# Attention with relative bias and a low-rank mixer: value products of the first three groups woven between scores in a new order, batch 0's remainder loads cast on the way, padding set sooner

## Chip, cores, metric

The kernel runs on one core of a Trainium2 chip. The metric is device microseconds of one execution. A comparison always has the kernel before beside it on the same chip, in alternating rounds.

## The reference, cut to what matters

```python
# q, k, v: (8 batches, 8 heads, 576 positions, 64)
scores = scale * q @ k^T + bias_table[bucket(|i - j|)]      # bucket saturates at distance 128
attn   = exp(scores - max) / (sum + 1e-9)
x      = (attn @ v) as (batch, 576, 512)
h      = (x^T @ U @ V)^T ;  u = x + h                        # U: (576, 32), V: (32, 576)
out    = u + relu(u @ w_ch1) @ w_ch2                         # 512 -> 2048 -> 512
```

The kernel treats two heads as a "pair" and one pair of one batch as a "group": group 0 to 3 are batch 0, group 4 begins batch 1. The 576 positions are four tiles of 128 and a remainder of 64. The bias is a factor exp(bias), read from table rows that only matter near the diagonal.

## The kernel before: the parts that count here

The main loop starts at group 4 and interleaves attention with the two large products of earlier batches. In front of it stands a prologue, written by hand, for batch 0. In the timelines of this document each engine runs its instructions in the order in which the program emits them, so one that waits holds all that stand behind it.

```python
def kts(g, *ks):          # scores of key tiles ks, then ScalarE's exponentials of them
def rem_scores(g):        # scores with the remainder of q and of k
def bands(g, *ks):        # VectorE: multiply the near-diagonal part by exp(bias)
def pvs(g, *ks):          # value products of both heads; ks=4 is the remainder and opens the sum
def normalise(g):         # VectorE: divide by the row sums, into x
def mix_t(g, copy), mix_ut(g, copy)     # x^T U, and u transposed
def first_transposes(pr, srcs, copies): # TensorE: 8 + 8 transposes of a pair's q and k, two copies out
def warm(n):              # n idle products of the identity
...
# loads on GpSimd, in this order, behind the table rows 0:
load_eb(0, nc.gpsimd)                        # waits until the table row is written
load_rem(0, 2)                               # v of batch 0: remainder,
for t in range(NKT): load_main(0, 2, t)      #   four tiles of 128 KB
qk0[3] = [first_qk(which, 3) for which in range(2)]      # pair 3's q and k
...
# the prologue, middle part
rem_scores(1)
more_loads()                                 # first of it: load_eb(3) on the SP queue
bands(0, 4, 0, 1, 2, 3)
kts(1, 2); warm(3); kts(1, 3)
reverse_eb(1); bands(1, 4, 0, 1, 2, 3)
rem_scores(2); kts(2, 0)
pvs(0, 4, 0, 1); kts(2, 1)
pvs(0, 2);       kts(2, 2)
pvs(0, 3); normalise(0); kts(2, 3)
first_transposes(3, qk0.pop(3), (nc.vector.tensor_copy, nc.scalar.copy))   # pair 3
first_rem_transposes(3)
pvs(1, 4, 0); rem_scores(3); pvs(1, 1, 2, 3); normalise(1); kts(3, 0)
...
```

The softmax here doesn't subtract the row's maximum and nothing guards it: scores larger than these inputs give would overflow.

## Time and profile before

| | |
|---|---|
| time | 392.95 us median of 3 (392.76 to 394.05) |
| TensorE busy | 96% of the span, 84% of the chain that ended last |
| VectorE, ScalarE, GpSimd busy | 76%, 52%, 33% |
| first remainder score of group 4 (the loop's start) | 35.58 us |
| span of the profiled execution | 392.6 us, granted clock 0.993 |

The busy shares are those of the whole span and say nothing about the prologue, which is 9% of it. To read the prologue, take each engine's timeline from 0 to 40 us: the bracket behind a line gives the idle time before it and who ended it. The lines are in the prediction.

### The profile page before, as it was taken

The page shows a single profiled execution, that of the slowest core. Times are in us where ns is not written, and L with a number is a line of the kernel's source. Part 1 is how long each engine was busy: PE and PEld are TensorE (multiplying, and loading weights), DVE is VectorE, ACT ScalarE, POOL GpSimd, SP SyncE. Part 2 cuts the span into 40 slices and gives each one's busy share as a digit, 9 for nine tenths or more (in the row PEclk, how much of TensorE's full clock was granted, in tenths as well). Part 3 has the DMA queues.
Part 4 walks back from the last instruction along what each step waited for, and adds up shares of the span by engine and source line. Part 5 has one row for each costly group of instructions (what it writes and reads, how often), then busy time and mean ns, then how long its engine had stood idle before and what let it go on. Part 6 is the DMA issues. An engine that isn't in the chain of part 4 may idle for free.

```text
span 392.6 us, 10145 instructions
## 1 busy us (share of the span) xinstructions
PE 376.6 (96%) x4126; PEld 250.9 (64%) x4161; DVE 299.6 (76%) x659; ACT 205.9 (52%) x312; POOL 129.5 (33%) x187
## 2 busy tenths in 40 slices
PE   7789999999999999999999999999999999999995
PEld 5366555555568656875588557855687569568474
DVE  7856898878897788877887888767876897465573
ACT  5977555565655676546755655566545650220310
POOL 4998917554554055404550335213000000000000
PEclk9989999999999999999999999999999999999998
DMA  7999999999999599978999798979003003401103
GB/s 135 180 96 168 158 202 115 135 102 140 179 80 96 124 160 84 106 131 148 105 82 134 145 110 65 141 140 142 3 16 122 15 15 28 121 1 55 53 2 107
DMA packets 163478, 40.66 MB, mean 104 GB/s; under 512 B 151568, under 2 KB 159032, under 8 KB 163432
## 3 DMA queue, kind: packets, MB, share of 16 engines
q0 software_dynamic: 110304, 18.24, 63.9%
q1 hardware_dynamic: 51864, 20.86, 25.4%
q10 hardware_dynamic: 1264, 0.92, 1.0%
q8 instruction: 32, 0.52, 0.5%
q14 instruction: 14, 0.11, 0.1%
HBM read 37.84 MB, written 9.45 MB: 120 GB/s over the span
## 4 chain that ended last, share of the span: by engine, by line
PE 84%; DVE 10%; ACT 2%; issue 1%; DMA 1%; SPq 0%; ACTq 0%; DVEq 0%
PE acc L410 28%; PE acc L539 26%; PE o L801 11%; PE sc L707 8%; PE acc L462 3%; DVE g L421 3%; PE acc L874 2%; PE sc L725 2%; DVE p_sb L777 2%; PE sc L746 1%; PE acc L681 1%; DMA stage<-in_q_dram 1%; DVE qkT L650 1%; DVE xp L827 1%; PE o L854 1%
## 5 line engine op out<-in xcount | busy, mean ns | idle before, releaser
L716 ACT ACTIVATE p_sb<-sc 128x1024 bf16<-128x1024 f32 (+1 forms) x125 | 120.3, 1015 | 97.2 <-PE sc L707 97.1
L410 PE MATMUL acc<-uT,w1b 128*128 128x512 bf16 x481 | 115.8, 380 | 2.2 <-issue 0.8
L410 PEld LDWEIGHTS <-w1b 128*128 128x128 bf16 x576 | 53.1, 98 | 68.7 <-issue 13.4
L421 DVE TENSOR_SCALAR g<-acc 128x512 f16<-128x512 f32 x97 | 64.8, 685 | 10.5 <-PE acc L410 9.6
L777 DVE TENSOR_TENSOR p_sb<-p_sb,eb 128x768 bf16<-128x768 bf16 (+4 forms) x156 | 65.5, 454 | 0.3 <-ACT p_sb L716 0.3
L801 PEld LDWEIGHTS <-p_sb 128*128 128x128 bf16 x1550 | 54.2, 98 | 4.8 <-issue 1.4
L539 PEld LDWEIGHTS <-g 128*128 128x128 f16 x512 | 48.7, 98 | 12.1 <-issue 5.5
L801 PE MATMUL o<-v_bf,p_sb 128*128 128x65 bf16 x1475 | 56.1, 193 | 0.3 <-DVE xp L827 0.3
L419 ACT ACTIVATE g<-acc 128x512 f16<-128x512 f32 x47 | 28.1, 598 | 46.3 <-PE acc L410 45.6
L539 PE MATMUL acc<-w2b,g 128*128 128x256 f16 x384 | 47.0, 273 | 0.1
L707 PE MATMUL sc<-qkT 64*128 64x512 bf16 x256 | 40.6, 385 | 1.4 <-ACT p_sb L716 0.9
L1147 POOL COPY gate<-xp 1x2 bf16<-1x2 bf16 x18 | 3.9, 214 | 114.3 <-DVE xp L827 114.3
L827 DVE TENSOR_TENSOR xp<-o,rcp 128x320 bf16<-128x320 f32 x60 | 29.5, 492 | 3.2
L539 PE MATMUL acc<-tw,stage 128*128 128x256 f16 x256 | 31.7, 273 | 0.0
L426 DVE TENSOR_TENSOR ob<-acc,u_tok 128x512 f32<-128x512 f32 x28 | 19.3, 688 | 13.5 <-PE acc L539 13.4
L275 POOL DMA_DIRECT2D v_bf<-in_v_dram x32 | 28.4, 926 | 0.3 <-issue 0.3
L882 DVE TENSOR_TENSOR u_tok<-acc,xp 128x512 bf16<-128x512 f32 x32 | 22.0, 686 | 8.5 <-PE acc L874 8.3
L539 PEld LDWEIGHTS <-stage 128*128 128x128 f16 x256 | 24.6, 98 | 4.0 <-issue 1.3
L558 DVE TENSOR_TENSOR ob<-acc,ob 128x512 f32<-128x512 f32 (+1 forms) x25 | 16.7, 667 | 11.6 <-PE acc L539 11.5
L757 ACT ACTIVATE p_sb<-sc 128x640 bf16<-128x640 f32 x31 | 21.7, 699 | 0.3 <-PE sc L749 0.3
L738 ACT ACTIVATE p_sb<-sc 128x512 bf16<-128x512 f32 x31 | 18.5, 597 | 4.1 <-PE sc L921 1.0
L275 POOL DMA_DIRECT2D qb<-in_k_dram x20 | 18.2, 909 | 1.6 <-issue 1.6
(126 smaller groups left out, 450.5 us busy)
## 6 DMA issues: line engine op xcount, KB each, us to landing
out_dram<-ob SPq DMA_DIRECT2D x16, 512.0 KB, 2.8
v_bf<-in_v_dram POOLq DMA_DIRECT2D x32, 128.0 KB, 5.6
qb<-in_q_dram POOLq DMA_DIRECT2D x23, 128.0 KB, 4.1
qb<-in_k_dram POOLq DMA_DIRECT2D x23, 128.0 KB, 4.2
w1b<-in_moe_w_ch_dram POOLq DMA_DIRECT2D x4, 512.0 KB, 7.0
w2b<-in_moe_w_ch_dram POOLq DMA_DIRECT2D x2, 1024.0 KB, 14.3
qb<-in_q_dram POOLq DMA_DIRECT2D x10, 64.0 KB, 5.5
qb<-in_k_dram POOLq DMA_DIRECT2D x10, 64.0 KB, 4.1
```

The costliest lines, as they stand in the source:

```text
L275: nc.gpsimd.dma_start(out=dst, in_=src[b, :, t * 128 : (t + 1) * 128, :].rearrange("h p d -> p h d"),)
L410: nc.tensor.matmul(gp_, lhsT=w1b[:, ct, nt * 128 : (nt + 1) * 128], rhs=rhs[:, ct, :], start=(ct == 0), stop=(ct == 3),)
L419: nc.scalar.activation(g[:, nt, :], gp_, AF.Relu)
L421: nc.vector.tensor_relu(out=g[:, nt, :], in_=gp_)
L539: nc.tensor.matmul(ps, lhsT=left[a](n)[:, t * 128 : t * 128 + 128], rhs=right[b](n), start=first and n == 0, stop=n == 7, skip_group_check ...
L707: nc.tensor.matmul(sp[:, hh, :], lhsT=kT[rows, i * 128 : (i + 1) * 128], rhs=qT[rows, 0:S0], start=True, stop=True,)
L716: nc.scalar.activation(P[:, i, hh, 0:S0], sp[:, hh, :], AF.Exp, scale=scale)
L757: nc.scalar.activation(P4[:, 0:SP], sp.rearrange("p a c -> p (a c)")[:, 0:SP], AF.Exp, scale=scale,)
L777: nc.vector.tensor_tensor(out=t, in0=t, in1=e, op=ALU.mult)
L801: nc.tensor.matmul(o[:, qt * 66 : qt * 66 + 65], lhsT=lhs[:, c0 : c0 + 128], rhs=rhs, start=(kt == NKT and qt == 0), stop=(kt == NKT - 1), ...
L827: nc.vector.tensor_tensor(out=xo[:, :, hh], in0=o[:, :, 0:64], in1=rbc, op=ALU.mult)
L882: nc.vector.tensor_tensor(out=u_tok[b % 3][:, pr, :, :], in0=hm.rearrange("p (t c) -> p t c", t=4), in1=x[:, 0:4, :], op=ALU.add,)
```

## The change

Its intent: let value products stand where TensorE waited for exponentials, take four VectorE casts and two fp32 loads out of the start, and put padding memsets on GpSimd in a wait it had anyway. The diff, cut to its core:

```diff
     first_load(1, 0, 2, k00, nc.scalar)
-    first_rem_load(0, nc.sync)
-    first_rem_load(1, nc.scalar)
     nc.scalar.activation(gmT[:, 0:1], negt31, AF.Exp)
     qk0[1] = [first_qk(which, 1) for which in range(2)]
+    load_rem(0, 0)
+    load_rem(0, 1)
     qk0[2] = [first_qk(which, 2) for which in range(2)]
@@
-    load_eb(0, nc.gpsimd)
+    load_eb(0)
@@
     setup_rest()
+    nc.gpsimd.dma_start(out=gate, in_=gp_dram[0:1, 0:2])
     load_rem(0, 2)
@@ casts and the order
     kts(0, 2, 3)
-    first_rem_cast(0)
-    first_rem_cast(1)
     first_transposes(2, qk0.pop(2), one)
...
     kts(1, 2)
-    warm(3)
     kts(1, 3)
+    pvs(0, 4, 0)
+    first_transposes(3, qk0.pop(3), (nc.vector.tensor_copy, nc.scalar.copy))
     reverse_eb(1)
-    bands(1, 4, 0, 1, 2, 3)
+    bands(1, 4, 0, 1, 2)
+    pvs(0, 1, 2, 3)
+    normalise(0)
+    band(1, 3)
     rem_scores(2)
     kts(2, 0)
-    pvs(0, 4, 0, 1)
     kts(2, 1)
-    pvs(0, 2)
+    pvs(1, 4, 0, 1)
     kts(2, 2)
...  (groups 2 and 3 likewise one place sooner; normalise(2) before the last bands)
```

More of the change, by code (lines that the diff above doesn't have):

```diff
@@ L106 @@
     scr = [t.rearrange("p a c -> p (a c)").bitcast(FP32) for t in tw]
-    rem_st = [
-        scr[2][:, w * 256 : w * 256 + 256].rearrange("p (a d) -> p a d", a=NPAIR)
-        for w in range(2)
-    ]
     gp = scr[1][0:8, 640 : 640 + GW // 2].bitcast(BF16)
@@ L202, with load_eb @@
     ebr = {}
-    def load_eb(pr, dma=nc.sync):
+    def load_eb(pr):
         t = stg.tile([128, 512], FP32, name="stage").bitcast(BF16)
@@ L207, in load_eb @@
         if pr < NPAIR:
-            dma.dma_start(
+            nc.sync.dma_start(
                 out=t[:, 0:768].rearrange("p (h c) -> p h c", h=2),
@@ L312, in load_rem @@
             nc.gpsimd.dma_start(out=dst[rows, :, par, 0:64], in_=vr[par])
-    def first_rem_load(which, dma):
-        vr = (q, k)[which][0, :, S0:S, :].rearrange("(a two) p d -> two p a d", two=2)
-        for par in range(2):
-            rows = slice(par * 64, par * 64 + 64)
-            dma.dma_start(out=rem_st[which][rows], in_=vr[par])
-    def first_rem_cast(which):
-        dst = rem_heads(rem[0][which])
-        for par in range(2):
-            rows = slice(par * 64, par * 64 + 64)
-            nc.vector.tensor_copy(out=dst[rows, :, par, :], in_=rem_st[which][rows])
     held = []
@@ L1057 @@
     first_rem_transposes(2)
+    first_rem_transposes(3)
     reverse_eb(0)
@@ L1062 @@
     kts(1, 2)
-    warm(3)
     kts(1, 3)
+    pvs(0, 4, 0)
+    first_transposes(3, qk0.pop(3), (nc.vector.tensor_copy, nc.scalar.copy))
     reverse_eb(1)
-    bands(1, 4, 0, 1, 2, 3)
+    bands(1, 4, 0, 1, 2)
+    pvs(0, 1, 2, 3)
+    normalise(0)
+    band(1, 3)
     rem_scores(2)
     kts(2, 0)
-    pvs(0, 4, 0, 1)
     kts(2, 1)
-    pvs(0, 2)
+    pvs(1, 4, 0, 1)
     kts(2, 2)
-    pvs(0, 3)
-    normalise(0)
+    pvs(1, 2, 3)
+    normalise(1)
+    mix_t(0, nc.scalar.copy)
     kts(2, 3)
-    first_transposes(3, qk0.pop(3), (nc.vector.tensor_copy, nc.scalar.copy))
-    first_rem_transposes(3)
-    pvs(1, 4, 0)
-    rem_scores(3)
-    pvs(1, 1, 2, 3)
-    normalise(1)
-    kts(3, 0)
-    mix_t(0, nc.scalar.copy)
-    kts(3, 1)
     reverse_eb(2)
@@ L1087 @@
     reverse_eb(3)
+    rem_scores(3)
+    kts(3, 0)
+    mix_t(1, nc.scalar.copy)
+    pvs(2, 4, 0)
+    kts(3, 1)
+    pvs(2, 1, 2, 3)
+    normalise(2)
     kts(3, 2)
-    mix_t(1, nc.scalar.copy)
-    pvs(2, 4, 0, 1)
     last = score(3, 3, True)
@@ L1093 @@
         post()
-    pvs(2, 2, 3)
+    bands(3, 4, 0, 1)
     mix_ut(0, nc.scalar.copy)()
     to_copy = fourth_transposes()
-    bands(3, 4, 0, 1)
-    normalise(2)
     for kt in (4, 0, 1):
```

## The prediction

> **What bounds the kernel now.** I first took the page's chain that ended last, to see which part of the span the change can touch. All edits lie before the main loop, so I then read the timeline of each engine over the first 38 us, and last the DMA issues with their times to landing. The main loop belongs to TensorE:
>
> ```profile
> PE 84%; DVE 10%; ACT 2%; issue 1%; DMA 1%; SPq 0%; ACTq 0%; DVEq 0%
> ```
>
> In the list of waits from 35 to 120 us no wait of TensorE on a DMA appears, and the loop's instructions and their order are unchanged. So a shift of the loop's start should be a shift of the end, one for one. The loop starts with the first remainder score of group 4:
>
> ```profile
> 35.58 0.40 PE L725 MATMUL sc<-qkT 128*128 128x128 bf16 x4 [0.27 <-ACT qkT L695]
> ```
>
> The question is whether 35.58 us moves. In the prologue ScalarE paces: one group (pair of heads) needs exponentials of 0.50 + 0.60 + 4 x 0.93 = 4.8 us (starts 15.01, 15.64, 16.24 and 1.94 for two), four groups 19.2 us, in the 28 us from 7.90 to 35.98. Its idle time is what a new order can win:
>
> ```profile
> 18.88 0.70 ACT L757 ACTIVATE g<-sc 128x640 bf16<-128x640 f32 x1 [0.21 <-PE sc L749]
> 19.48 1.02 ACT L716 ACTIVATE g<-sc 128x1024 bf16<-128x1024 f32 x1
> 21.73 2.85 ACT L716 ACTIVATE g<-sc 128x1024 bf16<-128x1024 f32 x3 [1.23 <-PE sc L707]
> 24.45 0.61 ACT L650 COPY qkT<-acc 128x512 bf16<-128x512 bf16 x1
> 25.68 0.60 ACT L738 ACTIVATE p_sb<-sc 128x512 bf16<-128x512 f32 x1 [0.62 <-ACT qkT L650]
> ...
> 33.58 0.58 ACT L915 CAST uT<-acc 128x512 bf16<-128x512 f32 x1 [1.30 <-PE o L801]
> ```
>
> The brackets give the idle time before a line and who ended it. With 0.22, 0.27 and 0.23 at 13.93, 27.14 and 30.55 us, these sum to 4.1 us. The 1.23 us is TensorE doing the value products of group 0 ahead of a score, and the last 1.30 is the tail of group 3.
>
> The lines I think decisive are the loads of the fourth pair's q and k and the place where they are used:
>
> ```profile
> 10.51 1.28 POOL L312 DMA_DIRECT2D v_bf<-in_v_dram  x2
> 11.75 3.56 POOL L275 DMA_DIRECT2D v_bf<-in_v_dram  x4
> 15.24 0.77 POOL L248 DMA_DIRECT2D qb<-in_q_dram  x1
> 15.93 0.78 POOL L248 DMA_DIRECT2D qb<-in_k_dram  x1
> ```
>
> ```profile
> qb<-in_k_dram POOLq DMA_DIRECT2D x1, 128.0 KB, 6.1
> ```
>
> ```profile
> 23.12 0.64 PE L646 MATMUL acc<-ident,qb 128*64 128x128 bf16 x16
> ```
>
> The middle line is from the DMA view around 16.5 us: that k lands 6.1 us after its issue begins, at 15.93 + 6.1 = 22.0; the q takes 5.6, landing at 20.8. The transposes at 23.12 wait for neither. Slack is only 1.1 us.
>
> **What the Trainium skill says.** "TensorE: Matmul & The Clock Gate", section "Step-by-step: what each phase is for": matmuls stay in program order, only weight loads are pulled ahead. The trace agrees: TensorE's timeline follows the program. So a transpose whose input has not landed holds every product behind it. The same page, section "What's actually happening": the array's clock falls to half when activity was low over a window of about 3.4 us, and rises after a busy one. The trace agrees: granted clock 0.58 and 0.56 in the stretches 18 to 20 and 20 to 22 us, 1.00 on both sides, and five value products cost 0.27 us there against 0.15 at 25 us. "Perfetto Trace Analysis", section "DMA Instruction — SWDGE (GPSIMD)": the recorded end of such an issue is the end of descriptor generation, not of the data. The trace agrees: 0.78 us of issue against 6.1 us to landing. "DMA: Bandwidth & Descriptors", section "Issuing engines are not separate DMA queues": moving a DMA between queues saves only issue time. So I give no gain in bandwidth to table rows 0 leaving GpSimd for the SP queue; no run yet shows it.
>
> **The change part by part.**
> (a) The remainder q and k of batch 0 no longer come as fp32 and through four VectorE casts (10.35 to 11.92, 1.57 us). Four casting loads go on GpSimd between the loads of pairs 1 and 2. At 0.63 us each (rows of the same shape at 23.0 us) they push pair 2's issues by 2.5 us, from 2.98 and 3.69 to 5.5 and 6.2. In the kernel before these landed at 8.8 and 9.4 amid heavy traffic; I estimate 4 to 4.5 us to landing now, so 9.6 and 10.5. Their transposes start at 10.21, so up to 0.4 us of wait. Against that, VectorE is free 1.57 us sooner and the remainder scores of group 0 no longer wait for it, which removes ScalarE's 0.22 us at 13.93. About zero.
> (b) The load of table rows 0 on GpSimd (9.24, 0.73 us) is replaced by a tiny gated DMA, still held until the table row is written at about 9.2. Its issue I estimate at 0.5 us from vpad's 0.50. The 0.6 us of padding memsets now fit into the idle wait before it. So v starts at 9.8 instead of 10.5, and pair 3's k is issued at about 15.2 and lands, at the same 6.1, at about 21.3; its q at 20.1. Rows 0 go third on the SP queue, at about 10.4, landing near 15.9 by the 5.5 us of the row at 10.37: in time for the bands that begin at 16.44.
> (c) The order. After group 1's last scores (about 17 us) the new program does ten + ten value products of group 0 (0.6 to 1 us), then pair 3's transposes, at about 17.9 us, 5 us sooner than before. Their load has gained 0.7 us. So TensorE stands from about 17.9 to 20.1, does eight transposes, and stands again until 21.3. ScalarE, with the exponentials of group 1 done at about 17.6, has the copy of that k next and then scores that stand behind it: it idles some 3.8 to 4.3 us.
> Then, from 21.3: eight transposes 0.45 us, forty value products 1.2 us (2.2 at half clock), the first four remainder scores 0.3 (0.5 at half clock). Group 2's first exponential starts between 23.2 and 24.5, against 18.05 now. TensorE idled most of the window before, so I expect half clock for much of this.
> From there the new order is good: products follow scores that ScalarE already has. Work left for ScalarE: 2 x 4.8 for groups 2 and 3, 0.5 for three small copies, 1.1 for two turns of u, 1.2 for the two copies of q and k = 12.4 us. Following the buffers (two score tiles, one o, three accumulators) I count small idles of 0.1, 0.15, 0.35 between scores and 0.8 at the tail, 1.4 in all. The loop begins 13.8 us later: 37.0 to 38.3, against 35.58. Sum: +1.4 to +2.7 us, middle +2.1.
> (d) The warm-up products dropped (three) were 0.3 us in an idle place: nothing by themselves.
>
> **The rivals.**
> *No stall: the load lands early enough or the weave hides it.* For it: the weave is sound, VectorE is lighter, the four idles of 1.23, 0.62, 0.27 and 0.23 us would mostly go. By the same counting without a stall the first exponential of group 2 starts about 20.2 (the copy and the products now come first) and the loop at 34.9, a gain of 0.6; with all four idles gone, 2.0 us. That is 391.0 to 392.3. Against it: the 6.1 us to landing. Tiny loads issued at 18.1 us still take 4.6 us, so the queue is backed up, and only 0.7 us of earlier issue is in sight.
> *The clock becomes the larger loss.* With an idle window before 21.3 us TensorE runs at half clock from then for up to 3.4 us, and some of group 2's later products double as well: 396 to 397. For it: the fall at 18 us in the kernel before came after less idleness. Against it: some products will run in the shadow of exponentials.
> *The stall is hidden.* ScalarE had 4.1 us of idle time after 13.9; if the wait only replaced it, and the tail shrank too, the time would be the same, 392.5 to 393.5. For it: the new order has little other idle time. Against it: my count leaves 1.4 us of the old idles and adds the products between the copy and the first score.
>
> **Range and chances.** Stall with 8 in 10: around +2, give or take 1. No net loss with 2 in 10: around -0.8. I put the time at 394.8 us, range 392.2 to 396.8. A change of 2% is 7.9 us: a gain of that size exceeds all 4.1 us of ScalarE's idle time, and a loss would need more than three times my stall. So 0.01, 0.97, 0.02.
>
> **What would show it.** Right: in the changed profile pair 3's transposes start on TensorE with a wait of 2 us or more released by the load of q or k in pair 3, in the stretch 17.5 to 22; ScalarE's exponentials pause there about 4 us; granted clock near 0.5 after it; later waits of ScalarE small; first remainder score of group 4 at 37 to 38. The remainder's loads land before 10 us and pair 2's transposes wait less than 0.5 us. Wrong: those transposes run without a wait because the loads land by 18 us, or the loop's start at 35 or sooner, or a start that moves without the end.

## The result

The changed kernel takes 397.59 us in the median (396.95 to 398.28, 4 runs) against 392.86 (392.4 to 394.05, 4 runs) in the same rounds. The ratio is 1.0116, 95% interval 1.0086 to 1.0146. A ratio here is the mean time of one kernel's runs over the mean of the other's of the same rounds, so it is not quite the ratio of the medians. The change loses 4.7 us, outside the range on record (392.2 to 396.8).

First TensorE's timeline of the changed kernel, as far as it answers to the lines of before:

```profile
18.12 0.31 PE L785 MATMUL o<-v_bf,p_sb 128*128 128x65 bf16 x5 [1.02 <-DMA v_bf<-in_v_dram]
18.27 0.32 PE L785 MATMUL acc<-v_bf,p_sb 128*128 128x65 bf16 x5
22.01 1.32 PE L630 MATMUL acc<-ident,qb 128*64 128x128 bf16 x16 [3.43 <-DMA qb<-in_q_dram]
23.26 0.46 PE L785 MATMUL o<-v_bf,p_sb 128*128 128x65 bf16 x5
...
24.90 0.62 PE L709 MATMUL sc<-qkT 128*128 128x128 bf16 x4
...
39.74 0.40 PE L709 MATMUL sc<-qkT 128*128 128x128 bf16 x4 [0.26 <-ACT qkT L679]
```

Pair 3's sixteen transposes stood at 23.12 us before and waited for nothing. Now they come up at 18.6 and wait 3.43 us for the load of q. The first remainder score of group 2 stands behind them and behind six sets of value products, at 24.90. In the kernel before, this score and ScalarE's first exponential of it stood at:

```profile
17.31 0.38 PE L725 MATMUL sc<-qkT 128*128 128x128 bf16 x4 [0.52 <-ACT p_sb L716]
18.05 0.62 ACT L738 ACTIVATE g<-sc 128x512 bf16<-128x512 f32 x1
```

The loop starts at 39.74, which is 4.16 us later than in the profile of before; the spans, 396.5 and 392.6, differ by 3.9. So the loss is all in the prologue.

What ScalarE makes of it, on its timeline:

```profile
16.14 1.94 ACT L700 ACTIVATE p_sb<-sc 128x1024 bf16<-128x1024 f32 x2
23.37 0.59 ACT L634 COPY qkT<-acc 128x512 bf16<-128x512 bf16 x1 [5.29 <-PE acc L630]
25.56 0.60 ACT L722 ACTIVATE g<-sc 128x512 bf16<-128x512 f32 x1 [1.60 <-PE sc L709]
26.09 0.70 ACT L741 ACTIVATE g<-sc 128x640 bf16<-128x640 f32 x1
```

It stands 5.29 us before its copy of that k, and 1.60 us more until the first score of group 2 is there. Before, the whole of its idle time in this part was 4.1 us, in seven pieces.

The clock, in stretches of 2 us (busy time and number of instructions of TensorE, weight loads, VectorE, ScalarE and GpSimd; then the granted clock, the DMA share and GB/s); first the kernel before, then the changed one:

```profile
16.00:18.00 2.00, 1.10 (x11) 0.70 (x10) 2.00 (x8) 2.00 (x3) 1.96 (x4) 1.00 2.33 157
18.00:20.00 2.00, 1.77 (x17) 0.89 (x17) 2.00 (x6) 1.79 (x4) 1.76 (x4) 0.58 1.39 208
20.00:22.00 2.00, 2.00 (x33) 1.47 (x30) 0.55 (x2) 0.77 (x2) 1.79 (x3) 0.56 1.27 92
22.00:24.00 2.00, 1.76 (x35) 1.04 (x31) 1.17 (x4) 2.00 (x3) 1.71 (x3) 1.00 1.16 75
```

```profile
20.00:22.00 2.00, 0.00 (x0) 0.00 (x0) 0.00 (x0) 0.00 (x0) 1.33 (x3) 0.76 0.79 65
22.00:24.00 2.00, 1.95 (x30) 1.54 (x31) 1.31 (x4) 0.59 (x1) 2.00 (x4) 0.50 1.16 75
24.00:26.00 2.00, 2.00 (x26) 1.49 (x24) 1.93 (x7) 0.44 (x1) 2.00 (x4) 0.50 1.27 80
26.00:28.00 2.00, 1.82 (x19) 0.90 (x19) 0.77 (x2) 1.94 (x4) 2.00 (x4) 0.53 0.81 56
```

TensorE does nothing at all from 20 to 22 us, and works at half clock for almost all of the next 6. Note the trap in the busy column: at half clock TensorE looks busier, not slower (2.00 of 2 us for 26 instructions from 24 us).

If the clock is either full or half, as the stretches at 1.00 and 0.50 suggest, a stretch of 2 us at 0.58 holds (1 - 0.58) / 0.5 x 2 = 1.7 us of half clock. Added up, that is 3.4 us in the kernel before and 6.8 us in the changed one. In the eight other profiles of the experiments that show half clock between 14 and 30 us the same sum gives 3.4 us (`order_only`, `eb3_late`, `eb3_again`, `filler_eb3`) or 6.8 us (`after_again`, `rows0_pool`, `ft3_late`, `pair3_first`): one or two windows of the 3.4 us that the prediction quotes.

The loads, on GpSimd's timeline and on the SP queue's. Against before, v is issued 0.67 us sooner (9.84, was 10.51), pair 3's k 0.68 us sooner (15.25, was 15.93), and table rows 3, the last of the four rows on the SP queue, near 13.2 us instead of near 15.8:

```profile
9.84 1.27 POOL L308 DMA_DIRECT2D v_bf<-in_v_dram  x2
11.07 3.57 POOL L271 DMA_DIRECT2D v_bf<-in_v_dram  x4
14.57 0.77 POOL L244 DMA_DIRECT2D qb<-in_q_dram  x1
15.25 0.79 POOL L244 DMA_DIRECT2D qb<-in_k_dram  x1
```

```profile
10.12 3.40 SPq L204 DMA_DIRECT2D stage<-gp_dram  x4
```

And the time from issue to landing of that k, from the DMA view at 15.5 us:

```profile
qb<-in_k_dram POOLq DMA_DIRECT2D x1, 128.0 KB, 7.4
```

So it lands at 15.25 + 7.4 = 22.65 us, and the q, issued at 14.57 with 7.4 too, at 21.97: later than before (22.03 for k, 20.84 for q), though issued sooner.

### The profile page after: what moved, and what is told of

The parts are those of the page before. It is cut to its first block, busy times and chain, and to the rows that moved or that the text cites. A ratio compares the mean times of both kernels' runs of the same rounds, so it can differ in the third digit from the quotient of the medians. Undisturbed runs are those within 1.5% of the kernel's fastest.

```text
span 396.5 us, 10173 instructions
## 1 busy us (share of the span) xinstructions
PE 380.2 (96%) x4158; PEld 252.6 (64%) x4158; DVE 299.0 (75%) x655; ACT 206.1 (52%) x312; POOL 131.7 (33%) x191
## 4 chain that ended last, share of the span: by engine, by line
PE 85%; DVE 8%; DMA 2%; ACT 2%; POOL 1%; issue 1%; ACTq 0%; DVEq 0%; POOLq 0%
PE acc L394 28%; PE acc L523 25%; PE o L785 11%; PE sc L691 8%; PE acc L446 3%; DVE g L405 3%; DMA qb<-in_q_dram 2%; PE acc L858 2%; PE sc L709 2%; DVE p_sb L761 1%; PE sc L730 1%; PE acc L665 1%; PE o L838 1%; POOL v_bf L271 1%; DMA gp_dram<-tw 1%
## 5 line engine op out<-in xcount | busy, mean ns | idle before, releaser
L394 PE MATMUL acc<-uT,w1b 128*128 128x512 bf16 x512 | 119.8, 380 | 0.1
L405 DVE TENSOR_SCALAR g<-acc 128x512 f16<-128x512 f32 x97 | 64.8, 685 | 10.5 <-PE acc L394 9.6
L410 DVE TENSOR_TENSOR ob<-acc,u_tok 128x512 f32<-128x512 f32 x28 | 19.3, 689 | 13.5 <-PE acc L523 13.3
L722 ACT ACTIVATE p_sb<-sc 128x512 bf16<-128x512 f32 x31 | 18.6, 599 | 3.7 <-PE sc L905 1.0
```

What stands on the lines that cost most here:

```text
L394: nc.tensor.matmul(gp_, lhsT=w1b[:, ct, nt * 128 : (nt + 1) * 128], rhs=rhs[:, ct, :], start=(ct == 0), stop=(ct == 3),)
L405: nc.vector.tensor_relu(out=g[:, nt, :], in_=gp_)
```

## The experiments

Theory A: the order puts pair 3's transposes where their data has not landed, and everything in program order behind them waits; the half clock after it is a cost of its own. Theory B: the new loads cost the time, the order is sound. Where an experiment's ratio is given, the kernel before is in the same rounds; the changed kernel stands at 1.0116, and at 1.0104 when it was timed again.

### 1 and 2. The order alone, the loads alone

`order_only`: the kernel before with the new order (its own loads and casts kept). `loads_only`: the changed kernel with the old order.

```diff
 # order_only, against the changed kernel
-    load_rem(0, 0); load_rem(0, 1)
+    first_rem_load(0, nc.sync); first_rem_load(1, nc.scalar)
-    load_eb(0)
+    load_eb(0, nc.gpsimd)
-    nc.gpsimd.dma_start(out=gate, in_=gp_dram[0:1, 0:2])
+    first_rem_cast(0); first_rem_cast(1)
 # loads_only: the middle part of the prologue as before, without the two first_rem_cast
```

> The new order of the program with the loads of the kernel before (fp32 remainder loads, four VectorE casts, table rows 0 on GpSimd, no gate). Theory A (the order alone moves pair 3's transposes to where their q and k have not landed): the transposes wait to about 20.8 us for q and 22.0 for k, as these landed in the kernel before; the loop starts between 38.5 and 39.7; time +3 to +4 us over before (396 to 397). Theory B (the new loads cause the loss, the order is sound): within 1 us of before.

> The new loads (casting remainder loads, gate, table rows 0 on the SP queue, no VectorE casts) with the old order. Theory A: pair 3's transposes, at about 23 us, find their data (22.0 and 22.7 in the changed kernel), so the time is that of before within 1 us, perhaps 0.3 us less for the casts. Theory B: +3 us or more.

Measured: `order_only` 396.95 us (396.67 to 397.93), ratio 1.0105 (1.0075 to 1.0136). `loads_only` 392.79 us (392.73 to 393.67), ratio 0.9997 (0.9973 to 1.0022). With the old loads and the new order TensorE waits like this:

```profile
20.66 0.41 PE L646 MATMUL acc<-ident,qb 128*64 128x128 bf16 x8 [2.87 <-DMA qb<-in_q_dram]
21.71 0.64 PE L646 MATMUL acc<-ident,qb 128*64 128x128 bf16 x8 [0.64 <-DMA qb<-in_k_dram]
```

With the new loads and the old order (`loads_only`) there is hardly a wait:

```profile
22.19 0.41 PE L630 MATMUL acc<-ident,qb 128*64 128x128 bf16 x8
22.78 0.41 PE L630 MATMUL acc<-ident,qb 128*64 128x128 bf16 x8 [0.17 <-DMA qb<-in_k_dram]
```

The order alone brings nearly all of the loss, the loads alone bring none. Theory B falls. (The new order includes the three warm-up products that it drops; they were not tested alone.) One number of Theory A's expectation missed: the loop started at 38.27, a little sooner than the 38.5 to 39.7 expected.

### 3. Pair 3's transposes put back late

```diff
     pvs(0, 4, 0)
-    first_transposes(3, qk0.pop(3), (nc.vector.tensor_copy, nc.scalar.copy))
...
     kts(2, 3)
+    first_transposes(3, qk0.pop(3), (nc.vector.tensor_copy, nc.scalar.copy))
     reverse_eb(2)
```

> The changed kernel with pair 3's transposes put back behind the last score of group 2. Theory A: the stall for q and k goes; the next data to be waited for are the v tiles of group 0's products, the last of which I put at 21.3 us (issued at 13.7, 7.6 to landing). So the first remainder score of group 2 comes at about 22 us instead of 24.9, the loop starts between 36 and 37.5, time 393.5 to 395.5: about 3 us of the 4.7 back. If the half clock is the larger part of the loss and the wait is not, less than 1.5 us comes back.

Measured: 396.04 us (395.56 to 396.91), ratio 1.0077 (1.0051 to 1.0103). A quarter to a third of the loss comes back (1.0077 against 1.0104 and 1.0116), not the 3 us I expected. TensorE's timeline tells why:

```profile
17.18 0.31 PE L785 MATMUL o<-v_bf,p_sb 128*128 128x65 bf16 x5 [0.92 <-DMA v_bf<-in_v_dram]
18.05 0.31 PE L785 MATMUL o<-v_bf,p_sb 128*128 128x65 bf16 x5 [0.41 <-DMA v_bf<-in_v_dram]
18.86 0.44 PE L785 MATMUL o<-v_bf,p_sb 128*128 128x65 bf16 x5 [0.35 <-DMA v_bf<-in_v_dram]
20.29 0.43 PE L785 MATMUL o<-v_bf,p_sb 128*128 128x65 bf16 x5 [0.72 <-DMA v_bf<-in_v_dram]
```

Each of the four full value tiles is used the moment it lands, and group 2's scores still stand behind the last of them. The first remainder score of group 2 comes at 20.81, where I expected about 22, and the loop starts at 37.38, near the upper end of what I expected. Half clock lasted 6.8 us here too (0.60, 0.50, 0.50 and 0.69 in the stretches from 18 to 26 us). And the expected times set the loop's start in the changed kernel's profile (39.74) against the median of 397.59, while that profile was of the slowest of its four runs (398.28 us).

### 4. Pair 3's loads ahead of v

```diff
+    qk0[3] = [first_qk(which, 3) for which in range(2)]
     load_rem(0, 2)
     for t in range(NKT):
         load_main(0, 2, t)
-    qk0[3] = [first_qk(which, 3) for which in range(2)]
```

> The changed kernel with pair 3's q and k issued ahead of the v tiles on GpSimd. Theory A in its wider form (the queue serves in order at a fixed rate, so any early use of what is loaded in this stretch waits): q and k land by 17, but the v tiles land about 1.4 us later each, the last at about 22.7; the wait moves to the value products and the time stays within 1 us of the changed kernel. Rival (only q and k were late, v has slack): the loop starts at about 36, time 393 to 394.5.

Measured: 395.44 us (394.65 to 396.46), ratio 1.0061 (1.003 to 1.0092). Between the two expectations, about 2 us below the changed kernel. Four of the five value tiles (the remainder is one) now wait 0.86, 0.61, 0.28 and 0.82 us for their loads, the last until 21.17, and ScalarE's first exponential of group 2 comes at 22.89. With 3 it shows that the wait is not for one late transfer: whatever of this stretch of the queue is used first is waited for. The four runs stand at two levels: 396.14 and 396.46 us at a clock of 0.990 and 0.989, 394.65 and 394.73 at 0.996 and 0.993. So part of the spread goes with the clock; whether a longer wait caused both, single runs can't tell.

### 5. Keeping TensorE busy while it waits

```diff
+    fill = ps_s.tile([128, 2, 512], FP32, name="sc")
+    for _ in range(64):
+        nc.tensor.matmul(fill[:, 0, 0:128], lhsT=ident, rhs=ident, start=True, stop=True)
     first_transposes(3, ...)
```

> The changed kernel with 64 idle products on a spare score tile ahead of pair 3's transposes, so that TensorE is busy while it would stand waiting. Theory: the half clock after the stall is a cost of its own. Granted clock 1.00 through 18 to 30 us (0.50 there in the changed kernel); the data still lands at 22 to 22.7; group 2's first exponential at 24.2 to 24.7 instead of 25.56, the loop's start 1.2 to 1.8 us sooner, time 395.8 to 396.4. Rival (the clock's loss lies in the shadow of other waits): less than 0.5 us.

Measured: 395.67 us (395.36 to 396.56), ratio 1.0069 (1.0043 to 1.0094), clock 0.998 to 1.000 in all five runs. The same stretches as above:

```profile
22.00:24.00 2.00, 1.59 (x36) 1.18 (x33) 1.97 (x7) 1.35 (x3) 2.00 (x4) 1.00 1.50 93
24.00:26.00 2.00, 1.80 (x37) 1.16 (x34) 1.29 (x4) 2.00 (x3) 2.00 (x4) 1.00 0.94 59
```

From the landing of k to group 2's first exponential it takes 23.09 - 21.40 = 1.69 us at full clock and 25.56 - 22.65 = 2.91 us at half clock. The rest of the way to the loop takes 36.84 - 23.09 = 13.75 us against 14.18. Together the profiles put 1.22 + 0.43 = 1.65 us on the half clock. The ratio of the timed runs agrees: it fell by 0.0035 to 0.0047, 1.4 to 1.8 us. (In this profile the k landed 1.25 us sooner than in the changed kernel's, and the loop began at 36.84; such spread between single profiles is why I take the size from the timed runs.) So of the 4.1 to 4.6 us lost, the half clock is a third or a little more, the wait the rest. The filler's runs and the changed kernel's are of different rounds, each set against the kernel before, so this share is not exact.

### 6 to 9. Why the load lands so late: rows 3 and rows 0

`eb3_late`: `load_eb(3)`, the table rows of pair 3, on GpSimd instead of the SP queue, so it is issued behind the loads of batch 1's first pair, at 25.56 us. `rows0_pool`: `load_eb(0, nc.gpsimd)` again and no gate. `after_again` is the changed kernel unaltered, `eb3_again` is `eb3_late` beside it on one chip.

> The changed kernel with only table rows 3 issued later, on GpSimd behind group 1's loads instead of at 13.2 us on the SP queue. Theory: these rows (192 KB), now issued 2.6 us sooner than in the kernel before, are carried ahead of pair 3's k and are why it lands at 22.7 and not at 21.3. Then q and k land about 0.7 to 1.1 us sooner (21.0 and 21.7) and the time falls by as much, to about 396.6. Rival (the backlog is of v and pair 3 alone): landing and time unchanged within 0.3 us.

> The changed kernel with table rows 0 back on GpSimd ahead of v and the gate taken out: part b undone alone. Theory (the order of transfers only decides who waits): v and pair 3 are issued 0.2 us later than in the changed kernel, rows for the first bands land later again (about 15), rows 3 are issued later too, and pair 3's k lands at 22.0 as in the kernel before: time 0 to 0.8 us less than the changed kernel. Rival (the gate is what costs): more than 1 us less.

> The changed kernel itself once more, for a second profile and for a comparison on the same chip with the next ones. Theory (the loss is a wait for data that lands at 20.5 to 22.7, which varies from run to run, plus one half-clock window after it): ratio 1.0105 to 1.0125; pair 3's transposes start between 20.5 and 22.2; clock near 0.50 for about 3.4 us after that.

> Late table rows 3 once more, beside the changed kernel on one chip. If issuing these rows early is what delays pair 3: 0.8 to 1.3 us below the changed kernel again and transposes at 20.5 to 21.2. If the first result was chance: within 0.4 us of it.

| run | median us | ratio (95%) | pair 3's transposes begin |
|---|---|---|---|
| changed kernel | 397.59 | 1.0116 (1.0086 to 1.0146) | 22.01 |
| after_again | 397.30 | 1.0104 (1.0086 to 1.0122) | 21.70 |
| rows0_pool | 397.31 | 1.0105 (1.0077 to 1.0133) | 21.04 |
| eb3_late | 396.31 | 1.0082 (1.0056 to 1.0108) | 20.50 |
| eb3_again | 396.34 | 1.0087 (1.0066 to 1.0108) | 19.87 |

Putting rows 0 back does not matter. With rows 3 late, the two profiles have the transposes 1.2 to 2.1 us sooner and the medians are 1.0 to 1.3 us lower, in two sets of rounds; but each time the intervals overlap those of the changed kernel, and the wait of a single profile scatters by a microsecond. There is a rival too: both profiles with rows 3 late have 3.4 us of half clock, the two of the changed kernel 6.8 (`after_again` was expected to have about 3.4). Among the runs with a clock of 0.991 or less, five with rows 3 late average 396.63 us and nine of the changed kernel 397.41 (pooled over rounds), so some 0.8 us remains at a like clock. I take rows 3 for a likely part of the late landing, not for a settled one.

### 10 and 11. Both repairs at once

`filler_eb3`: late rows 3 and 48 filler products. `filler80_eb3`: the same with 80.

> The changed kernel with 48 idle products ahead of pair 3's transposes and with table rows 3 issued late: both part repairs at once. If the loss is the sum of a wait for data and of the half clock after it, the gains add: 1.8 us of the filler and 1.3 us of the late rows, so 394.3 to 395.0, ratio about 1.004, clock 1.00. If they are the same loss seen twice, it stays at 395.5 or above.

> Both repairs with 80 filler products instead of 48, which ended at 18.9 us, 2.6 us before the data. Theory: the filler now reaches the landing, the clock stays at 1.00, and the time is at most that of the first filler (395.7), and 394.5 to 395.2 if late rows 3 really bring the data sooner.

Measured: 396.02 us (395.43 to 397.03), ratio 1.0077 (1.0057 to 1.0097), and 396.62 us (395.96 to 398.26), ratio 1.0092 (1.0068 to 1.0115). Both miss; the gains do not add. In the first profile the 48 products ended near 19.3 us, the q came at 21.48, and the clock fell to 0.58 and 0.56 between 22 and 26 us: an idle gap of 2.2 us. In the second the clock stays at 1.00, but the products themselves take until 22.7, so they, and not the data, hold the transposes:

```profile
18.09 4.63 PE L1051 MATMUL sc<-ident 128*128 128x128 bf16 x80
```

So these two say nothing firm on the sum; a filler whose length must match a wait that scatters by a microsecond is a poor repair.

### 12. A weave that uses nothing early

```diff
-    pvs(0, 4, 0); first_transposes(3, ...); reverse_eb(1); bands(1, ...); pvs(0, 1, 2, 3); normalise(0)
-    rem_scores(2); kts(2, 0); kts(2, 1); pvs(1, 4, 0, 1); kts(2, 2); ...
+    reverse_eb(1); bands(1, 4, 0, 1, 2, 3)
+    rem_scores(2); kts(2, 0); pvs(0, 4); kts(2, 1); pvs(0, 0, 1); kts(2, 2)
+    first_transposes(3, qk0.pop(3), one)            # both copies on VectorE
+    pvs(0, 2, 3); normalise(0); kts(2, 3); rem_scores(3)
+    ... group 3's scores between group 1's products; the changed kernel's last part
```

> A version meant to beat both: the new loads, group 2's scores again ahead of all value products but one tile's, pair 3's transposes behind the third score tile of group 2 (at about 22 us, both copies on VectorE), its remainder scores directly behind group 2's scores, and the new tail. Theory: with nothing used before it lands, ScalarE idles less than 2 us between 17.6 us and the loop's start, which comes at 33 to 34.3; time 391 to 392.3. If VectorE's order (nine products and copies between 23 and 34 us) is the next bound, the start is at 34.5 to 35 and the time that of before.

Measured: 393.94 us (392.98 to 395.53), ratio 1.0024 (0.9998 to 1.0051). ScalarE waits 0.84 us at most for a score, but the loop starts at 34.47 in the fastest of its runs, with ScalarE waiting 1.69 and 0.86 us for the turned u of groups 0 and 1; just before, TensorE waits 0.97 us for VectorE's x of group 1: the second case of the expectation, as far as one profile shows. With group 2's scores in front again, most of the loss is gone while the change's loads stay in place. As a version it is no better than the kernel before.

### 13 and 14. The two levels of the kernel before

Of 49 timed runs of the kernel before in the experiments' rounds 12 are above 393.5 us; nine of these have a granted clock of 0.991 to 0.994. `before_warm` adds 18 warm-up products between 15 and 18 us; `before_again` is the kernel before, profiled once more.

> The kernel before with 18 more warm-up products after group 1's third and fourth scores and after its remainder scores (9 instead of 3, 9 more, 3 more), in places where TensorE waited about 0.5 us. Theory: the two levels at which the kernel before runs (spans near 390.8 at clock 1.00, near 392.3 at 0.993 to 0.994) differ by one half-clock window in the prologue, and the fuller stretch before 18 us keeps it away: all runs near 392.5 to 393.0 with clock 0.998 or more, none near 394. Rival (the levels come from elsewhere, in the main loop or the transfers): still some runs near 394, or all shifted up by the added products.

> The kernel before, for a second profile. If this execution is at the upper of its two levels (span near 392.3) its profile shows a half-clock window in the prologue as the first one did; if at the lower (span near 390.8), none, and the loop starts near 34.0 instead of 35.6.

Measured: `before_warm` 393.44 us (392.75 to 394.17), ratio 1.0012 (0.9992 to 1.0033), clock 0.997 or more in all six runs: no half-clock window, as expected, but three runs between 393.7 and 394.2 all the same, which was not. (Their spans are 391.8, 392.1 and 391.3 us, so the last lost its time outside the profiled span.) `before_again` took 394.59 us at clock 0.999, span 392.8, and shows why. Its loop starts at 34.49, 1.1 us sooner than in the first profile, and yet it ends no sooner:

```profile
46.99 0.39 PE L410 MATMUL acc<-uT,w1b 128*128 128x512 bf16 x1 [1.34 <-DMA w1b<-in_moe_w_ch_dram]
```

In the main loop TensorE waits 1.34 us for the third quarter of the first weight, issued at 39.96 here and at 39.19 in the first profile. So the slow executions of the kernel before are of at least two kinds: a half-clock window in the prologue (the first profile), and loads that run behind the loop (the second).

### 15 to 17. A version that beats both

`tail_copies`: `loads_only`, and ScalarE's two copies of group 4's q and k ahead of its copy of group 1's u. `tail_w1`: that, and `load_w1(2)` issued ahead of batch 1's v. `before_w1`: the kernel before with only the latter.

```diff
     normalise(2)
+    for copy in to_copy:
+        copy()
     for kt in (4, 0, 1):
         pv(3, kt, (0,))
...
         load_w1(1)
+        load_w1(2)
         load_rem(1, 2)
```

> A second try at beating both: the new loads with the old order, and ScalarE's two copies of group 4's q and k moved ahead of its copy of group 1's u, into the 1.3 us in which it waits there. Theory: the first remainder score of group 4 no longer waits for these copies but for TensorE's own work before it, 0.3 to 0.5 us sooner; time 392.1 to 392.5 in runs at full clock. If the later copies of u and of the small product then hold TensorE, the time is that of before.

> The new loads with the old order and ScalarE's copies moved ahead, as in the second try, and the third quarter of the first weight issued before batch 1's v instead of behind its third pair. Theory: an earlier start of the loop was eaten by a wait of TensorE for this quarter (0.2 us at 45 us in the second try, 1.3 us in the second profile of the kernel before); with it gone the loop's gain arrives at the end: 391.6 to 392.3, no wait on that quarter in the profile, interval below 1.000. Rival: batch 1's v or the pair loads, now later, are waited for instead: 392.5 or above.

> The kernel before with the third quarter of the first weight issued before batch 1's v, nothing else. Theory: of its runs above 393.5 those at clock 0.998 or more (two of some 35 so far) come from that wait and vanish; those at 0.991 to 0.994 come from a half-clock window and stay; the lower level stays at 392.4 to 392.8. Rival (the quarter always costs something): the lower level falls by 0.3 us or more.

Measured: `tail_copies` 392.61 us (391.75 to 393.14), ratio 0.9987 (0.9968 to 1.0007): not shown faster. Its loop starts at 33.60, and it then waits 0.22 us for the weight. `tail_w1` 392.17 us (391.77 to 392.42), ratio 0.9985 (0.9973 to 0.9998): faster than the kernel before by 0.15%, with the interval just below 1, in one set of rounds. The loop starts without a wait, and no wait for the weight follows:

```profile
33.41 0.39 PE L709 MATMUL sc<-qkT 128*128 128x128 bf16 x4
```

`before_w1` 392.54 us (392.41 to 392.68), ratio 0.9996 (0.9982 to 1.0009): the lower level does not move, and none of its five runs is above 392.7. With nine half-clock runs in 49 of the kernel before, five without one prove nothing about that kind.

## Why the prediction was wrong

Its mechanism was right, and so was its direction. What failed is the size of two terms of its sum: the base, a loop start of 35.58 us taken from a slow execution while the shift was added to the median of others (1.4 us), and the time from issue to landing of pair 3's k, kept at 6.1 us where it was 7.4 (1.35 us in the profile). Either one taken from 397.59 gives about 396.2, inside the range. Point by point:

- **The stall** (part c): pair 3's transposes wait on TensorE for the load, ScalarE pauses (5.29 us, where I had said 3.8 to 4.3), the clock falls after it, later waits of ScalarE are small (0.24, 0.32, 0.25 us). Shown by the profile and by experiments 1 and 2. I missed that the value tile in front would wait too (1.02 us), which costs nothing while the later wait is longer.
- **The landing** (part b), a mis-sized term. The issue times came out as worked (9.8 and 15.2 predicted, 9.84 and 15.25 measured). I kept the 5.6 and 6.1 us to landing of before; it was 7.4 for both, so k landed at 22.65 and not 21.3: 1.35 us. The error was to carry a time to landing over to a queue whose other traffic the change reorders. Table rows 0 to 2 landed 4.3 to 4.7 us after issue and rows 3 were issued 2.6 us sooner, ahead of pair 3; experiments 6 to 9 make rows 3 a likely cause, without settling it.
- **From the landing to group 2's first exponential** (part c): 1.95 to 3.15 us predicted, 2.91 measured, so nearly all of it at half clock; against the middle of 2.55, 0.36 us. Here I had also counted forty value products where three tiles of two heads make thirty; at 0.27 us for five they took 1.64 us.
- **From there to the loop**: 13.8 us predicted, 39.74 - 25.56 = 14.18 measured; 0.38 us. The count was right at full clock: in the six profiles of the new order whose half clock lasted 3.4 us or not at all this stretch took 13.70 to 13.79 us (`order_only`, `eb3_late`, `eb3_again`, `filler`, `filler_eb3`, `filler80_eb3`). I had allowed for half clock of up to 3.4 us; it lasted 6.8. The three together are 2.1 us: 37.65, the middle of 37.0 to 38.3, plus 2.1 gives the 39.74. As that profile was of the slowest of four runs, 0.7 us above the median, some 1.4 of the 2.1 count in the medians.
- **The base** failed, and this is the step that I had not seen as a step at all. I took the loop's start of 35.58 from one profile and added the shift to the median of other runs, 392.95. That profile was of an execution of 394.37 us, 1.4 us longer, with a half-clock window (clock 0.993, span 392.6). Most executions of the kernel before have none, a span of 390.6 to 391.2, and a loop that starts near 34: 34.05 in the closely related `before_w1`, span 390.9, and 34.00 in `before_warm`, span 391.0; a profile of the kernel itself at that level I do not have. The clock line stood in front of me, 0.58 and 0.56, and I quoted it as a property of the kernel. Against 34.0 my own 37.0 to 38.3 would have been +3.0 to +4.3 us, that is 396 to 397.3.
- **One for one**: the spans less the loop's start are 357.0 us before, 356.8 in the changed kernel and 356.7 to 356.8 in `order_only`, `ft3_late` and `filler`. Right for a later start. Not always for an earlier one: it was 357.5 in `loads_only`, 357.7 in `tail_copies` and 358.3 in `before_again`, with waits of 0.26, 0.22 and 1.34 us on the weight, but 356.85 to 357.0 in `before_w1`, `before_warm` and `tail_w1`, which have no such wait.
- **The small parts** were about zero, as predicted: pair 2's transposes did not wait (loads of 3.4 and 3.5 us from 5.42 and 6.12, at 8.8 and 9.6; I had said 9.6 and 10.5), ScalarE's 0.22 us before the remainder of group 0 is gone, and `loads_only` is at 0.9997. The dropped warm-up products (part d) were not tested alone.
- **The rivals**: "no stall" is refuted by the profile. "The clock becomes the larger loss" gave the time nearest to the measured one, 396 to 397, but not for its reason: the clock is about a third of the loss (experiment 5). "The stall is hidden" is refuted. One sum among the rivals does not come out: 20.2 and the 13.8 us counted for the rest make 34.0, a gain of 1.6 us, not 34.9 and 0.6. The range did not rest on it.

The whole is then: the new order uses, at 17 to 19 us, data that lands at 18 to 22.65 us, and puts the scores that feed ScalarE behind that use. The wait makes about two thirds of the loss and half clock after it about one third; why k landed later than before is not settled.

## What to carry to other kernels

Before moving work ahead on an engine that runs in program order, write down for every operand when it lands, not when it is issued, and let the next work that feeds the pacing engine stand in front of anything that may wait. A time to landing belongs to a queue with its traffic; if the change reorders the traffic, give that term a range of its own. And look at what level the base profile is: if executions come in two levels, find the level of the profiled one before adding a shift to a median.

## What the Trainium skill lacked or had wrong

- "TensorE: Matmul & The Clock Gate", section "Why this matters for your kernels", advises against idle gaps above about 3 us. The trace shows less to be enough: in the kernel before the clock fell at about 18.3 us after waits of 0.53 us at most since 12 us, with TensorE busy 1.46 us of the 2 from 14 and 1.10 us of the 2 from 16; in `filler_eb3` it fell after a gap of 2.2 us. The page has no figure for how busy a window must be, nor for how many short idles are enough. Nor does the busy time alone decide it: `before_w1` had 1.45 and 1.10 us in the same stretches and kept full clock. Of 49 timed executions of the kernel before, nine have the lower mean clock (0.991 to 0.994), so a single profile can hold a fall or not.
- "DMA: Bandwidth & Descriptors", section "Anatomy of one DMA — SWDGE (gpsimd) path", gives 2.0 us plus the bytes over 436 GB/s, an estimate of 2.3 us for 128 KB, or 2.6 us for the 256 KB of fp32 that these converting loads read. The loads of 128 KB here took 3.4 to 3.5 us when issued at 5.42 and 6.12 us in the changed kernel, and 5.6 to 7.6 us behind v and the table rows (issued from 11 to 16 us). The page's fit has no term for what is queued ahead.
